# Attention and FFN on one core: softmax reciprocals turned one step later, two small jobs on GpSimd

## Chip, cores and metric

The program runs on one core of one Trainium2 chip. The metric is the device time of one execution in microseconds (us). Matmuls run on TensorE (PE; its weight loads are listed as PEld), elementwise work on VectorE (DVE), ScalarE (ACT) and GpSimd (POOL), transfers are issued by SyncE (SP).

## The reference, cut to what matters

```python
scores = scale * np.matmul(q, k.transpose(0, 1, 3, 2))        # batch 4, heads 8, seq 576, head 64
scores = scores + bias.transpose(2, 0, 1)[None]               # bias from a small MLP of the positions
scores = scores - np.max(scores, axis=-1, keepdims=True)
attn = np.exp(scores)
attn = attn / (np.sum(attn, axis=-1, keepdims=True) + 1e-09)
x = np.matmul(attn, v)                                        # -> 2304 tokens x 512
h = x @ w_in                                                  # 512 x 2048
return np.maximum(0.01 * h, h) @ w_out                        # 2048 x 512
```

## The kernel before

The program has three stages: the bias tables (to about 55 us), attention (to about 317 us) and the FFN. The change is in attention, which works on 16 units, one for each of 4 head pairs (`hp`) and 4 batches (`b`), in this order. A unit has nine tiles of scores, `KINDS = A0, B0, A1, B1, M, A2, B2, A3, B3`: A and B are the two heads, the digit a block of 128 queries, and M holds the last 64 queries of both heads. The order of everything is written out by hand: `step(n)` issues the work for tile n, and engines run their own instructions in that order.

For tile n of a step, `qk_mm` makes the scores on PE (L235, for M L227), `softmax_a` adds the bias and takes the row's extreme on DVE (L258, a custom instruction and a small one that reads its accumulator), and `softmax_b` takes the exponential and its row sum `sm` on ACT (L266). Three steps later (`LAG = 3`) `transposes` turns the tile on PE (L300; its last 128 columns go into a tile `ps_o`, L304 or L318), and ACT copies the result into `PT` (L316, L306).

The scaling by 1/(sum + 1e-9) comes last, since the product is computed transposed. `recip` runs once for each half of a unit, a step after M (half g = 0) and a step after B3 (half g = 1): DVE adds 1e-9 (L272), takes the reciprocal (L273), and GpSimd spreads it over columns in `rb` (L276, L278) and, for M, copies 64 columns of `pM` (L279). `turn_rb` turns `rb` on PE into columns 256 to 511 of `ps_o` (L289, for M also L305), and DVE copies it to `PT` (L290, for M before it two half copies, L309). `pv` is the product with V, 20 matmuls of half a unit (L335). It writes columns 0 to 287 of the same `ps_o` tile that L290 reads. `pv_exit` multiplies the product by the reciprocals on DVE (L344, L348).

In this text "the first turn" is `turn_rb` of half 0 and "the first product" the `pv` of half 0, which stands in the step of the next unit's A0; "the second turn" and "the second product" are those of half 1. The second product stands in the next unit's M step, where transposes and product go ahead of the scores (`ahead`); in all other steps the scores come first.

The FFN takes x in two parts, a rounded high part `xh` and the remainder `xl`. For the first block of 512 tokens, which are those of batch 0 (units 0, 4, 8 and 12, counted from 0), the split is made inside attention: ACT rounds as `pv_exit` runs (L345) and DVE subtracts one step later (L386). That is eight pieces, of 288 and 224 columns. Between these jobs GpSimd makes the low parts of q and k for the next unit (`split_lo`, L206 and L209), and DVE their high parts (L194, L199) and some of the weights' preparation (`fill`, L432 to L448).

Of the kernel before, what the change touches and what calls it, by code (L numbers as in the profile page):

```python
# [8 lines left out]
F32 = mybir.dt.float32  # L9
# [5 lines left out]
B, H, S, D, HID = 4, 8, 576, 64, 32  # L15
# [10 lines left out]
KINDS = ["A0", "B0", "A1", "B1", "M", "A2", "B2", "A3", "B3"]  # L26
# [3 lines left out]
LAG = 3  # L30
# [6 lines left out]
def attention_ffn(ctx: ExitStack, tc: tile.TileContext, qt, kt, vm, vt, wi, wo, cst, out):  # L37
    nc = tc.nc
# [18 lines left out]
    ident = ap.tile([128, 128], F32, name="ident")  # L57
# [7 lines left out]
    PT = ap.tile([128, 2, 10, HS], F32, name="PT")  # L65
# [27 lines left out]
    for T in GEN:  # L93
        w = gen_w(T)
# [116 lines left out]
    st, pp = {}, {}  # L211

    def tile_id(n):
        u, i = divmod(n, 9)
        return u, KINDS[i]
# [24 lines left out]
    def softmax_a(n):  # L240
        u, kind = tile_id(n)
        hp = u // B
        bt = bias[hp, "M"][:] if kind == "M" else bias[hp, kind[1]][:, 0 if kind[0] == "A" else 1, :]
        col = 1 if kind[0] == "B" else 0
        if col == 0:
            mx_t[n] = ap.tile([128, 2], F32, tag="mx", name="mx", bufs=6)
        else:
            mx_t[n] = mx_t[n - 1]
        g, sc = int(KINDS.index(kind) > 4), 4 if kind == "M" else 2 * (int(kind[1]) % 2) + col
        if kind in ("A0", "A2"):  # L250
            sm_t[u, g] = ap.tile([128, 12], F32, tag="sm", name="sm", bufs=3)
        if kind == "M":
            pair[0] = ap.tile([128, S + 64], F32, tag="pM", name="pM", bufs=1)
        elif col == 0:
            pair[0] = ap.tile([128, 2 * S], F32, tag="p", name="p", bufs=3)
        p = pair[0][:, S * col:S * col + S]
        s_, i = st.pop(n), mx_t[n][:, col:col + 1]
        nc.vector.tensor_tensor_reduce(out=p, in0=s_[:, S0:S0 + S], in1=bt, scale=-0.125, scalar=3.4e38, op0=ALU.add, op1=ALU.min, accum_out=i)  # L258
        pp[n] = pair[0]
        ex_q.append((p, i, sm_t[u, g][:, sc:sc + 1]))  # L260
# [3 lines left out]
    def softmax_b():  # L264
        p, i, sm = ex_q.pop(0)
        nc.scalar.activation(out=p, in_=p, func=AF.Exp, bias=i, scale=-1.0, accum_out=sm)  # L266

    def recip(n):
        u, kind = tile_id(n)
        g = int(kind != "M")  # L270
        sm, w = sm_t.pop((u, g)), 4 if g else 5
        nc.vector.tensor_scalar_add(sm[:, 0:w], sm[:, 0:w], 1e-9)  # L272
        nc.vector.reciprocal(sm[:, 6:6 + w], sm[:, 0:w])  # L273
        rb = rb_t[u, g] = ap.tile([128, 384], F32, tag="rb", name="rb", bufs=2)
        one = sm[:, 6:10].rearrange("p (h o) -> p h o", o=1).to_broadcast([128, 4, 64])
        nc.gpsimd.tensor_copy(rb[:, 0:256].rearrange("p (h c) -> p h c", h=4), one)  # L276
        if g == 0:
            nc.gpsimd.tensor_copy(rb[:, 256:384], sm[:, 10:11].to_broadcast([128, 128]))  # L278
            nc.gpsimd.tensor_copy(pp[n][:, S:S + 64], pp[n][:, S - 64:S])  # L279

    outs = {}
    pv_q = []

    def halves(t):
        return t[:].rearrange("p (a c) -> p a c", a=2)

    def turn_rb(u, g, rb):
        for i in range(2):
            nc.tensor.transpose(outs[u, g][:, 256 + 128 * i:384 + 128 * i], rb[:, 128 * i:128 * i + 128], ident[:])  # L289
        nc.vector.tensor_copy(PT[:, g, 8:10, 0:256], halves(outs[u, g]))  # L290

    def transposes(n, at):
        u, kind = tile_id(n)
        p = pp.pop(n)
        p0 = S + 64 if kind[0] == "B" else 0
        if kind in ("A0", "M"):
            outs[u, int(kind == "M")] = pstile("o")
        t0 = pstile("t")
        for jb in range(4):
            nc.tensor.transpose(t0[:, 128 * jb:128 * jb + 128], p[:, p0 + 128 * jb:p0 + 128 * jb + 128], ident[:])  # L300
        if kind == "M":
            rb = rb_t.pop((u, 0))
            tl = outs[u, 1]
            nc.tensor.transpose(tl[:, 0:128], p[:, 512:640], ident[:])  # L304
            nc.tensor.transpose(tl[:, 256:384], rb[:, 256:384], ident[:])  # L305
            nc.scalar.copy(out=PT[:, :, 0:8, 256:288], in_=t0[:].rearrange("p (j g c) -> p g j c", j=8, g=2))  # L306
            for h in range(2):
                r, c = slice(64 * h, 64 * h + 64), slice(64 * h, 64 * h + 64)
                nc.vector.tensor_copy(PT[r, :, 8:10, 256:288], halves(tl)[r, :, c].rearrange("p a (g c) -> p g a c", g=2))  # L309
            turn_rb(u, 0, rb)  # L310
            pv_q.append((at, u, 0))
            return
        ic, h = int(kind[1]), 0 if kind[0] == "A" else 1
        g, i2 = ic // 2, ic % 2
        c = slice(128 * i2, 128 * i2 + 128)
        nc.scalar.copy(out=PT[:, g, 0:8, c].rearrange("p (j h) c -> p j h c", h=2)[:, :, h, :], in_=t0[:].rearrange("p (j c) -> p j c", j=4))  # L316
        if h == 1:
            nc.tensor.transpose(outs[u, g][:, c], p[:, 512:640], ident[:])  # L318
            if kind == "B3":
                turn_rb(u, 1, rb_t.pop((u, 1)))  # L320
                pv_q.append((at, u, 1))

    x_pend, pv_out = [], []

# [13 lines left out]
    def pv_exit():  # L338
        hp, t0, o, r = pv_out.pop(0)
        c = max(0, min(HS, BLK - t0))  # L340
        if c:
            x = ap.tile([128, HS], F32, tag="xt", name="xt", bufs=2)
            hi, lo = (t[:, t0:t0 + c] for t in xs[0, hp])
            nc.vector.tensor_mul(x[:, 0:c], o[:, 0:c], r[:, 0:c])  # L344
            nc.scalar.copy(out=hi, in_=x[:, 0:c])  # L345
            x_pend.append((lo, x[:, 0:c], hi))
        if c < HS:
            nc.vector.tensor_mul(x1[hp][:, t0 + c - BLK:t0 + HS - BLK], o[:, c:HS], r[:, c:HS])  # L348

    NTILE = 9 * HP * B  # L350

# [13 lines left out]
    def step(n):  # L365
        ahead = n % 9 == 4
        for turn in (ahead, not ahead):
            if turn:
                if 0 <= n - LAG < NTILE:
                    transposes(n - LAG, n + 2)  # L370
                if pv_q and pv_q[0][0] <= n:
                    pv()
                continue
            if n < NTILE:
                qk_mm(n)
                if ahead and n // 9 + 2 < HP * B:
                    load_unit(n // 9 + 2)
                if ahead:
                    split(n, "M")
                    fill(n, 3)  # L380
                softmax_a(n)
            if 0 <= n - 1 < NTILE and KINDS[(n - 1) % 9] in ("M", "B3"):
                recip(n - 1)
            while x_pend:
                lo, x, hi = x_pend.pop(0)
                nc.vector.tensor_sub(lo, x, hi.bitcast(F32))  # L386
            while pv_out and not ahead:
                pv_exit()
        while ex_q:
            softmax_b()  # L390
# [258 lines left out]
```

## Time and profile before

| | |
|---|---|
| median of 3 runs (lowest to highest) | 720.21 us (719.26 to 720.31) |
| the profiled execution: time, span | 719.8 us, 718.0 us |
| busy share of the span: PE, PEld, DVE, ACT, POOL | 97%, 76%, 54%, 50%, 16% |
| granted TensorE clock, mean over the span | 1.000 of full speed |

The profile is of one execution. "Busy" is time in which an engine had an instruction under way; a PE matmul's end is modelled, so what counts for PE is where its instructions start. A remark in brackets behind a row, as [0.20 <-POOL pM L279], is idle time of that engine just before it, and what ended it.

### The profile page before, as it was taken

The numbers are of one execution on the slowest core, as the hardware profiler recorded it, in microseconds if no ns is written. First come the engines' busy times: TensorE is split into PE (matmuls) and PEld (weight loads), VectorE is DVE, ScalarE is ACT, GpSimd is POOL, SyncE is SP. The second block draws the span as 40 slices with busy tenths as digits, with TensorE's granted clock in tenths as the row PEclk, the third lists the DMA queues.
The fourth block names the chain that finished last, engine by engine and source line by source line (L and its number), as shares of the span: only waits on it lengthen the run. The fifth ranks groups of instructions, "written<-read, shape, count | busy, mean of one in ns | idle before, by whom it ended". The sixth has DMA issues, their size and how long they took to land.

```text
span 718.0 us, 11142 instructions
## 1 busy us (share of the span) xinstructions
PE 698.7 (97%) x4192; PEld 544.2 (76%) x4192; DVE 388.8 (54%) x882; ACT 362.6 (50%) x792; POOL 111.9 (16%) x135
## 2 busy tenths in 40 slices
PE   6999999999999999999999999999999999999997
PEld 2346677777767786767888888888888888888996
DVE  7996789898889889749996211122111221112111
ACT  7797778767778777775563221222211231122221
POOL 2103335333444434300000000000000000000000
PEclk9999999999999999999999999999999999999999
DMA  9798557447755864002550010000000010000100
GB/s 231 239 316 243 167 164 226 115 114 214 211 158 127 244 173 125 21 1 65 173 174 29 1 59 0 1 0 30 31 0 1 0 59 1 0 1 1 59 1 30
DMA packets 30262, 68.26 MB, mean 95 GB/s; under 512 B 8192, under 2 KB 8320, under 8 KB 30208
## 3 DMA queue, kind: packets, MB, share of 16 engines
q1 hardware_dynamic: 30208, 67.54, 32.4%
q8 instruction: 33, 0.54, 0.3%
q14 instruction: 21, 0.17, 0.1%
HBM read 51.92 MB, written 15.61 MB: 94 GB/s over the span
## 4 chain that ended last, share of the span: by engine, by line
PE 85%; DVE 9%; ACT 3%; issue 2%; DMA 1%; DVEq 0%; SPq 0%
PE ps_o L466 13%; PE ps_t L466 13%; PE ps_o L335 10%; PE ps_s L494 9%; PE ps_s L493 9%; PE ps_s L492 9%; PE ps_s L235 7%; PE ps_t L300 6%; DVE r L114 2%; PE ps_o L125 2%; PE ps_t L125 1%; DVE p L258 1%; PE ps_s L227 1%; PE ps_s L125 1%; DVE pM L258 1%
## 5 line engine op out<-in xcount | busy, mean ns | idle before, releaser
L481 DVE TENSOR_TENSOR gl<-g,gh 128x512 fp32r<-128x512 f32 (+1 forms) x80 | 51.0, 638 | 266.2 <-ACT g L475 266.2
L494 PE MATMUL ps_s<-woh,gl 128*128 128x512 f32 x288 | 112.1, 389 | 0.3 <-DVE gl L481 0.3
L492 PE MATMUL ps_s<-woh,gh 128*128 128x512 f32 x288 | 112.2, 390 | 0.0
L493 PE MATMUL ps_s<-wol,gh 128*128 128x512 f32 x288 | 112.2, 390 | 0.0
L266 ACT ACTIVATE p<-p,mx 128x576 f32<-128x576 f32 x128 | 100.0, 781 | 7.6 <-DVE mx L258 7.6
L258 DVE CUSTOM_DVE_ANT_0 p<-ps_s,bias 128x576 f32<-128x576 f32 x128 | 94.0, 750 | 15.0 <-PE ps_s L235 12.5
L235 PE MATMUL ps_s<-ks,qs 128*128 128x288 f32 x512 | 99.9, 318 | 1.8 <-DVE mx L258 1.5
L235 PEld LDWEIGHTS ps_s<-ks,qs 128*128 128x128 f32 x512 | 72.1, 189 | 19.5 <-issue 6.0
L474 ACT ACTIVATE gh<-ps_o 128x512 fp32r<-128x512 f32 (+1 forms) x39 | 21.5, 552 | 126.6 <-PE ps_o L466 126.6
L316 ACT COPY PT<-ps_t 128x512 f32<-128x512 f32 x128 | 73.4, 574 | 12.9 <-PE ps_t L300 12.9
L474 ACT ACTIVATE gh<-ps_t 128x512 fp32r<-128x512 f32 (+1 forms) x39 | 21.5, 552 | 112.0 <-PE ps_t L466 111.9
L300 PE MATMUL ps_t<-ident,p 128*128 128x128 f32 x512 | 75.0, 273 | 2.3 <-ACT PT L316 2.3
L335 PE MATMUL ps_o<-PT,v 128*64 128x288 f32 x512 | 69.2, 412 | 0.3
L300 PEld LDWEIGHTS ps_t<-ident,p 128*128 128x128 f32 x512 | 61.1, 140 | 4.5 <-ACT PT L316 3.6
L494 PEld LDWEIGHTS ps_s<-woh,gl 128*128 128x128 f32 x288 | 54.1, 188 | 12.0 <-DVE gl L481 0.7
L492 PEld LDWEIGHTS ps_s<-woh,gh 128*128 128x128 f32 x288 | 54.1, 188 | 10.8
L493 PEld LDWEIGHTS ps_s<-wol,gh 128*128 128x128 f32 x288 | 54.1, 188 | 10.6
L466 PE MATMUL ps_t<-xh,wil 128*128 128x512 f32 (+1 forms) x156 | 57.3, 367 | 0.0
L466 PE MATMUL ps_o<-xh,wil 128*128 128x512 f32 (+1 forms) x156 | 57.3, 367 | 0.0
L466 PE MATMUL ps_t<-xl,wih 128*128 128x512 f32 (+1 forms) x156 | 57.3, 367 | 0.0
L466 PE MATMUL ps_o<-xl,wih 128*128 128x512 f32 (+1 forms) x156 | 57.3, 367 | 0.0
L466 PE MATMUL ps_t<-xh,wih 128*128 128x512 f32 (+1 forms) x156 | 57.2, 367 | 0.0
(109 smaller groups left out, 1098.8 us busy)
## 6 DMA issues: line engine op xcount, KB each, us to landing
raw<-kt SPq DMA_DIRECT2D x32, 304.0 KB, 5.7
raw<-qt SPq DMA_DIRECT2D x32, 288.0 KB, 4.2
raw<-wi SPq DMA_DIRECT2D x16, 512.0 KB, 3.5
raw<-wo SPq DMA_DIRECT2D x16, 512.0 KB, 3.6
scr<-x SPq DMA_DIRECT2D x21, 295.5 KB, 4.2
bias<-scr SPq DMA_DIRECT2D x16, 288.0 KB, 5.4
out<-x SPq DMA_DIRECT2D x18, 256.0 KB, 2.1
v<-vm SPq DMA_DIRECT2D x16, 256.0 KB, 6.3
```

Source lines behind the costliest of these rows:

```text
L235: nc.tensor.matmul(s_[:, S0 + HS * hh:S0 + HS * hh + HS], qs[:, c0:c0 + 128], ks[:, k0 + HS * hh:k0 + HS * hh + HS], start=(j == 0), stop= ...
L258: nc.vector.tensor_tensor_reduce(out=p, in0=s_[:, S0:S0 + S], in1=bt, scale=-0.125, scalar=3.4e38, op0=ALU.add, op1=ALU.min, accum_out=i)
L266: nc.scalar.activation(out=p, in_=p, func=AF.Exp, bias=i, scale=-1.0, accum_out=sm)
L300: nc.tensor.transpose(t0[:, 128 * jb:128 * jb + 128], p[:, p0 + 128 * jb:p0 + 128 * jb + 128], ident[:])
L316: nc.scalar.copy(out=PT[:, g, 0:8, c].rearrange("p (j h) c -> p j h c", h=2)[:, :, h, :], in_=t0[:].rearrange("p (j c) -> p j c", j=4))
L335: nc.tensor.matmul(o[64 * h:64 * h + 64, 0:HS], l, r, start=(jb == 0), stop=(jb == 4))
L466: nc.tensor.matmul(h_[:, :N], w, x[:, :N], start=(j == 0), stop=(j == len(mms) - 1))
L474: nc.scalar.activation(out=gh[:, :N], in_=h_[:, :N], func=AF.Prelu, alpha=0.01)
L481: nc.vector.tensor_sub(gl[:, :N], g[:, :N], gh[:, :N].bitcast(F32))
L492: nc.tensor.matmul(o, gh[:, c], wt[m][2][:], start=(m == 0), stop=False)
L493: nc.tensor.matmul(o, gh[:, c], wt[m][3][:], start=False, stop=False)
L494: nc.tensor.matmul(o, gl[:, c], wt[m][2][:], start=False, stop=(m == MF - 1))
```

## The change

The addition of 1e-9 leaves DVE for GpSimd and gets a function of its own, `sums`, in the step in which it stood; the copy of the 64 columns of `pM` goes with it and so comes ahead of the spreading. `recip` (now the reciprocal and the spreading) runs two steps after M and B3 instead of one. `turn_rb` runs one step after the tile's other transposes instead of in the same step; the products keep their steps. For the first block, ACT's rounding moves to the next step (`x_steps`), and the subtraction goes from DVE to GpSimd, another step later.

```diff
@@ -265,18 +265,24 @@
         p, i, sm = ex_q.pop(0)
         nc.scalar.activation(out=p, in_=p, func=AF.Exp, bias=i, scale=-1.0, accum_out=sm)
 
+    def sums(n):
+        u, kind = tile_id(n)
+        g = int(kind != "M")
+        sm, w = sm_t[u, g], 4 if g else 5
+        nc.gpsimd.tensor_scalar_add(sm[:, 0:w], sm[:, 0:w], 1e-9)
+        if g == 0:
+            nc.gpsimd.tensor_copy(pp[n][:, S:S + 64], pp[n][:, S - 64:S])
+
     def recip(n):
         u, kind = tile_id(n)
         g = int(kind != "M")
         sm, w = sm_t.pop((u, g)), 4 if g else 5
-        nc.vector.tensor_scalar_add(sm[:, 0:w], sm[:, 0:w], 1e-9)
         nc.vector.reciprocal(sm[:, 6:6 + w], sm[:, 0:w])
         rb = rb_t[u, g] = ap.tile([128, 384], F32, tag="rb", name="rb", bufs=2)
         one = sm[:, 6:10].rearrange("p (h o) -> p h o", o=1).to_broadcast([128, 4, 64])
         nc.gpsimd.tensor_copy(rb[:, 0:256].rearrange("p (h c) -> p h c", h=4), one)
         if g == 0:
             nc.gpsimd.tensor_copy(rb[:, 256:384], sm[:, 10:11].to_broadcast([128, 128]))
-            nc.gpsimd.tensor_copy(pp[n][:, S:S + 64], pp[n][:, S - 64:S])
 
     outs = {}
     pv_q = []
@@ -284,12 +290,22 @@
     def halves(t):
         return t[:].rearrange("p (a c) -> p a c", a=2)
 
-    def turn_rb(u, g, rb):
+    def turn_rb(n, at):
+        u, kind = tile_id(n)
+        g = int(kind != "M")
+        rb = rb_t.pop((u, g))
+        if g == 0:
+            tl = outs[u, 1]
+            nc.tensor.transpose(tl[:, 256:384], rb[:, 256:384], ident[:])
+            for h in range(2):
+                r, c = slice(64 * h, 64 * h + 64), slice(64 * h, 64 * h + 64)
+                nc.vector.tensor_copy(PT[r, :, 8:10, 256:288], halves(tl)[r, :, c].rearrange("p a (g c) -> p g a c", g=2))
         for i in range(2):
             nc.tensor.transpose(outs[u, g][:, 256 + 128 * i:384 + 128 * i], rb[:, 128 * i:128 * i + 128], ident[:])
         nc.vector.tensor_copy(PT[:, g, 8:10, 0:256], halves(outs[u, g]))
-
-    def transposes(n, at):
+        pv_q.append((at, u, g))
+
+    def transposes(n):
         u, kind = tile_id(n)
         p = pp.pop(n)
         p0 = S + 64 if kind[0] == "B" else 0
@@ -299,16 +315,8 @@
         for jb in range(4):
             nc.tensor.transpose(t0[:, 128 * jb:128 * jb + 128], p[:, p0 + 128 * jb:p0 + 128 * jb + 128], ident[:])
         if kind == "M":
-            rb = rb_t.pop((u, 0))
-            tl = outs[u, 1]
-            nc.tensor.transpose(tl[:, 0:128], p[:, 512:640], ident[:])
-            nc.tensor.transpose(tl[:, 256:384], rb[:, 256:384], ident[:])
+            nc.tensor.transpose(outs[u, 1][:, 0:128], p[:, 512:640], ident[:])
             nc.scalar.copy(out=PT[:, :, 0:8, 256:288], in_=t0[:].rearrange("p (j g c) -> p g j c", j=8, g=2))
-            for h in range(2):
-                r, c = slice(64 * h, 64 * h + 64), slice(64 * h, 64 * h + 64)
-                nc.vector.tensor_copy(PT[r, :, 8:10, 256:288], halves(tl)[r, :, c].rearrange("p a (g c) -> p g a c", g=2))
-            turn_rb(u, 0, rb)
-            pv_q.append((at, u, 0))
             return
         ic, h = int(kind[1]), 0 if kind[0] == "A" else 1
         g, i2 = ic // 2, ic % 2
@@ -316,9 +324,6 @@
         nc.scalar.copy(out=PT[:, g, 0:8, c].rearrange("p (j h) c -> p j h c", h=2)[:, :, h, :], in_=t0[:].rearrange("p (j c) -> p j c", j=4))
         if h == 1:
             nc.tensor.transpose(outs[u, g][:, c], p[:, 512:640], ident[:])
-            if kind == "B3":
-                turn_rb(u, 1, rb_t.pop((u, 1)))
-                pv_q.append((at, u, 1))
 
     x_pend, pv_out = [], []
 
@@ -342,10 +347,20 @@
             x = ap.tile([128, HS], F32, tag="xt", name="xt", bufs=2)
             hi, lo = (t[:, t0:t0 + c] for t in xs[0, hp])
             nc.vector.tensor_mul(x[:, 0:c], o[:, 0:c], r[:, 0:c])
-            nc.scalar.copy(out=hi, in_=x[:, 0:c])
             x_pend.append((lo, x[:, 0:c], hi))
         if c < HS:
             nc.vector.tensor_mul(x1[hp][:, t0 + c - BLK:t0 + HS - BLK], o[:, c:HS], r[:, c:HS])
+
+    x_lo = []
+
+    def x_steps(n):
+        while x_lo:
+            lo, x, hi = x_lo.pop(0)
+            nc.gpsimd.tensor_sub(lo, x, hi.bitcast(F32))
+        while x_pend:
+            lo, x, hi = x_pend.pop(0)
+            nc.scalar.copy(out=hi, in_=x)
+            x_lo.append((lo, x, hi))
 
     NTILE = 9 * HP * B
 
@@ -367,7 +382,9 @@
         for turn in (ahead, not ahead):
             if turn:
                 if 0 <= n - LAG < NTILE:
-                    transposes(n - LAG, n + 2)
+                    transposes(n - LAG)
+                if 0 <= n - LAG - 1 < NTILE and KINDS[(n - LAG - 1) % 9] in ("M", "B3"):
+                    turn_rb(n - LAG - 1, n + 1)
                 if pv_q and pv_q[0][0] <= n:
                     pv()
                 continue
@@ -379,11 +396,11 @@
                     split(n, "M")
                     fill(n, 3)
                 softmax_a(n)
+            if 0 <= n - 2 < NTILE and KINDS[(n - 2) % 9] in ("M", "B3"):
+                recip(n - 2)
             if 0 <= n - 1 < NTILE and KINDS[(n - 1) % 9] in ("M", "B3"):
-                recip(n - 1)
-            while x_pend:
-                lo, x, hi = x_pend.pop(0)
-                nc.vector.tensor_sub(lo, x, hi.bitcast(F32))
+                sums(n - 1)
+            x_steps(n)
             while pv_out and not ahead:
                 pv_exit()
         while ex_q:
```

How this moves instructions shows at three places. The first is DVE's order around the second turn of one unit, in the next unit's steps B0 to M. `qs` and `ks` are the high parts of q and k, `x` the scaled product, `mx` the accumulator, `tmp` weights in preparation. Before:

```order
L348 TENSOR_TENSOR x_1_70<-ps_o,PT 128x288
L194 CAST qs_101<-raw_84 128x1024
L258 ISA p,mx<-ps_s,bias 128x576
L258 ISA mx 128x1
L290 COPY PT<-ps_o 128x2x256
L258 ISA p,mx<-ps_s,bias 128x576
L258 ISA mx 128x1
L199 CAST ks_2032<-raw_85 128x1216
```

The same place now, where the numbers of the lines are those of the changed file (L352 was L348, L305 was L290):

```order
L352 TENSOR_TENSOR x_1_70<-ps_o,PT 128x288
L194 CAST qs_101<-raw_84 128x1024
L258 ISA p,mx<-ps_s,bias 128x576
L258 ISA mx 128x1
L258 ISA p,mx<-ps_s,bias 128x576
L258 ISA mx 128x1
L305 COPY PT<-ps_o 128x2x256
L199 CAST ks_2032<-raw_85 128x1216
```

The copy of the reciprocals to `PT` has changed places with the softmax instruction of tile B1; the reciprocal of this half, which stood some instructions earlier, now stands just ahead of the first row.

The second place is PE's order around the same turn, from the scores of tile B1 to the product. Before, with the two transposes of `rb` ahead of those scores:

```order
L289 MATMUL ps_o<-ident,rb 128x128 x2
L235 MATMUL ps_s<-ks_2455,qs_101 128x288 x2
L235 MATMUL ps_s<-ks_2456,qs_101 128x288 x2
L300 MATMUL ps_t<-ident,p 128x128 x8
L318 MATMUL ps_o<-ident,p 128x128
L335 MATMUL ps_o<-PT,v 64x288 x8
```

And now (L316 was L300, L326 was L318, L304 was L289, L340 was L335):

```order
L235 MATMUL ps_s<-ks_2455,qs_101 128x288 x2
L235 MATMUL ps_s<-ks_2456,qs_101 128x288 x2
L316 MATMUL ps_t<-ident,p 128x128 x4
L304 MATMUL ps_o<-ident,rb 128x128 x2
L316 MATMUL ps_t<-ident,p 128x128 x4
L326 MATMUL ps_o<-ident,p 128x128
```

Between the turn and the product stood four matmuls of scores and nine transposes, and now five transposes; the row of the product follows.

The third place is GpSimd's order, from the M tile of one unit to the first piece of `xl` in the next but one step. Before:

```order
L276 COPY rb<-sm 128x256
L278 COPY rb<-sm 128x128
L279 COPY pM<-pM 128x64
L209 TENSOR_TENSOR ks_1621<-raw_85,ks_1620 128x576
L209 TENSOR_TENSOR ks_1621<-raw_85,ks_1620 128x640
L276 COPY rb<-sm 128x256
L206 TENSOR_TENSOR qs_100<-raw_82,qs_100 64x512 x2
```

And now:

```order
L272 TENSOR_SCALAR sm<-sm 128x5
L274 COPY pM<-pM 128x64
L209 TENSOR_TENSOR ks_1621<-raw_85,ks_1620 128x576
L283 COPY rb<-sm 128x256
L285 COPY rb<-sm 128x128
L209 TENSOR_TENSOR ks_1621<-raw_85,ks_1620 128x640
L272 TENSOR_SCALAR sm<-sm 128x4
L283 COPY rb<-sm 128x256
L206 TENSOR_TENSOR qs_100<-raw_82,qs_100 64x512
L359 TENSOR_TENSOR xl_902<-xt,xh_901 128x288
L206 TENSOR_TENSOR qs_100<-raw_82,qs_100 64x512
```

The spreading into `rb` has moved behind the first of the two pieces of k's low part, and the copy of `pM` ahead of it; the two additions and a subtraction are new on this engine.

## Rows read from the trace of the kernel before

**Rows 1.** Busy time by stretch, two units: us, then each engine, PEclk, DMA, GB/s.

```profile
117.74:133.51 15.77, 15.77 (x129) 12.23 (x130) 13.55 (x35) 12.58 (x31) 6.95 (x9) 1.00 0.72 207
133.51:151.31 17.80, 16.50 (x129) 12.23 (x130) 15.65 (x37) 12.60 (x31) 7.45 (x9) 1.00 0.51 126
```

**Rows 2.** Chain that ended last, products and one DVE piece: start, us, what.

```profile
117.74 2.58 PE ps_o L335 x20
...
124.30 2.58 PE ps_o L335 x20
...
133.51 2.58 PE ps_o L335 x20
...
139.26 1.15 DVE xl L386
...
141.07 2.65 PE ps_o L335 x20
...
151.31 2.58 PE ps_o L335 x20
```

**Rows 3.** Timeline around a second turn: start, us, engine, line, operation.

```profile
170.60 0.76 DVE L258 CUSTOM_DVE_ANT_0 p<-ps_s,bias 128x576 f32<-128x576 f32 x1 [1.24 <-PE ps_s L235]
...
171.29 0.45 DVE L348 TENSOR_TENSOR x<-ps_o,PT 128x288 f32<-128x288 f32 x1
...
171.66 0.68 DVE L194 CAST qs<-raw 128x1024 fp32r<-128x1024 f32 x1
...
172.25 0.75 DVE L258 CUSTOM_DVE_ANT_0 p<-ps_s,bias 128x576 f32<-128x576 f32 x1
...
172.93 0.68 DVE L290 COPY PT<-ps_o 128x512 f32<-128x512 f32 x1
...
173.75 1.17 PEld L335 LDWEIGHTS ps_o<-PT,v 128*64 128x64 f32 x12 [0.17 <-DVE PT L290]
```

**Rows 4.** Line L335, what its weight loads waited for: us, times.

```profile
  DVE PT L290: 3.9, 19
```

**Rows 5.** Timeline around a first turn.

```profile
113.66 0.17 DVE L272 TENSOR_SCALAR sm<-sm 128x5 f32<-128x5 f32 x1 [0.26 <-ACT pM L266]
...
114.18 0.40 POOL L276 COPY rb<-sm 128x256 f32<-128x256 f32 x1 [4.38 <-DVE sm L273]
...
114.75 0.24 POOL L279 COPY pM<-pM 128x64 f32<-128x64 f32 x1
...
114.95 2.96 POOL L209 TENSOR_TENSOR ks<-raw,ks 128x576 fp32r<-128x576 f32 x2
...
115.05 0.14 PEld L304 LDWEIGHTS ps_o<-ident,pM 128*128 128x128 f32 x1 [0.20 <-POOL pM L279]
...
115.44 0.56 PEld L235 LDWEIGHTS ps_s<-ks,qs 128*128 128x128 f32 x4
...
117.67 1.65 PEld L335 LDWEIGHTS ps_o<-PT,v 128*64 128x64 f32 x16 [0.17 <-DVE mx L258]
```

**Rows 6.** Groups by line and shape, 54 to 330 us: busy us, mean ns.

```profile
L209 POOL TENSOR_TENSOR ks<-raw,ks 128x576 fp32r<-128x576 f32 x15 | 21.4, 1428 | 0.0
...
L273 DVE RECIPROCAL sm<-sm 128x5 f32<-128x5 f32 x16 | 3.0, 189 | 0.5
```

**Rows 7.** Timeline, DVE instructions that overlap a GpSimd instruction.

```profile
147.65 1.58 DVE L386 TENSOR_TENSOR xl<-xt,xh 128x224 fp32r<-128x224 f32 x1
...
153.26 0.70 POOL L276 COPY rb<-sm 128x256 f32<-128x256 f32 x1 [2.60 <-DVE sm L273]
153.62 0.62 DVE L432 TENSOR_SCALAR tmp<-tmp 128x512 f32<-128x512 f32 x1
...
168.44 0.40 DVE L432 TENSOR_SCALAR tmp<-tmp 128x512 f32<-128x512 f32 x1
```

**Rows 8.** Timeline, a unit whose M tile comes late from DVE.

```profile
162.29 0.56 PEld L235 LDWEIGHTS ps_s<-ks,qs 128*128 128x128 f32 x4 [0.29 <-DVE mx L258]
```

**Rows 9.** Chain that ended last, the piece behind the last product.

```profile
322.70 0.68 DVE wil L448
```

## Prediction

> **What bounds the kernel now.** I read the busy time by stretch first, since the change lies in attention alone. A unit in the middle of attention, from one first product to the next, takes 15.77 us, and PE is busy in all of it [rows 1]. The unit behind it takes 17.80 us with PE busy for 16.50 us: it is one in which the first block's low parts are made. So a plain unit is set by PE's order, and an instruction that comes later on PE's way makes the unit longer, unless something else there gets shorter.
>
> The chain that ended last, read second, splits the units into two windows. Window A goes from the first product to the second, window B from the second to the next first. In the plain unit they take 124.30 - 117.74 = 6.56 us and 133.51 - 124.30 = 9.21 us [rows 2]. In the unit with the low parts they take 7.56 us and 10.24 us: 1.00 and 1.03 us more, with the subtraction (1.15 us) on the chain in the first. These pairs of windows come once for each head pair, so there are 4 x 2.03 = 8.1 us to be had from the low parts.
>
> The timeline around a second turn, read third, shows how close DVE is behind PE. DVE waits for the scores of tile B0 until 170.60, works without a pause through softmax, x, qs, softmax, and ends the copy of the reciprocals at 172.93 + 0.68 = 173.61; the product's first weight load starts at 173.75 [rows 3]. Elsewhere a product shows the same 0.17 us before its load where nothing binds, as in [rows 5], so here DVE's copy has some 0.08 us of slack. The product's loads waited for this copy 19 times, 3.9 us in all, 0.2 us each [rows 4]: a wait that is just met, not one with room. It can't be left out, because the product overwrites the columns that the copy reads.
>
> **The change, part by part.**
>
> *The second turn* is the largest term. On DVE the copy now stands behind the softmax of B1 instead of ahead of it, and the reciprocal, which stood earlier, now stands in this stretch. The softmax costs 172.93 - 172.25 = 0.68 us [rows 3]. The reciprocal's instruction lasts 0.19 us, but DVE's next one starts before it ends; I take 0.10 us (bounds 0.10 to 0.19) [rows 6]. With 0.08 us of slack the product starts 0.68 + 0.10 - 0.08 = 0.70 us later. PE has nothing to put there: its next instruction in order is the product itself, and behind it stand the M tile's scores.
>
> To this comes GpSimd's spreading, which follows the reciprocal and now runs as DVE comes to the cast of q (it ran earlier, beside the weights' work). The instruction of L432 takes 0.40 us alone and 0.62 us when a spreading started 0.36 us before it, and that spreading 0.70 us instead of 0.40 us; the subtraction L386, 224 columns, took 1.58 us beside a piece of k of 1.43 us [rows 5, 6, 7]. So each of the two engines can hold the other up. I take 0.15 us, with bounds of 0 (they miss each other) and 0.40 us (the whole spreading). The second turn then costs 0.70 + 0.15 = 0.85 us.
>
> The Trainium skill has a rule for this (SBUF — State Buffer, "Who interferes with whom"): of a GpSimd instruction and a DVE instruction in a mode that uses both ports, the one that starts first keeps the shared pair to its end and the other waits fully. The trace agrees with it in the 0.62 us of rows 7. By the rule alone, with the cast due about 0.16 us into the spreading, the wait would be an estimated 0.24 us rather than 0.15 us, and the time 0.9 us longer than mine.
>
> There are 15 second turns inside attention (the 16th is at the tail). Four are in windows with a low part; the one of the last unit but one has no cast of q beside it (there is no unit to prepare), and I give it 0.3 us. The other ten give 10 x 0.85 = 8.5 us.
>
> *The first turn* loses something and gains something. Before, PE waited 0.20 us for the copy of pM, which was third in GpSimd's queue [rows 5]. Now that copy is second, behind the addition, and is long done. PE also has three transposes less at that place, so the scores of B3 start at 115.44 - 0.45 = 114.99 (0.20 us of wait and 0.25 us of weight loads). But the spreading now stands behind a piece of k of 1.43 us [rows 6]. I reckon it through in the times of [rows 5]: the row sums of M are ready at about 113.6 (DVE's addition started at 113.66). GpSimd's addition has no row; the nearest is the copy of 64 columns, 0.24 us, and its bounds are 0.10 us (almost nothing) and 0.70 us (the longest spreading [rows 7]). Addition, copy and piece of k end at 113.66 + 0.24 + 0.20 + 1.43 = 115.53, and the two spreadings, 114.75 - 114.18 = 0.57 us, at 116.10. PE wants them at about 115.98 and turns them by 116.6. DVE's two half copies and the full copy behind them take 0.62 + 0.69 = 1.31 us, and so the product's load starts at 117.98 instead of 117.67. With the rounding of these rows I take 0.33 us, bounds 0.20 us (then the softmax of B3 sets DVE's start) and 0.79 us. All 16 first turns pay, four of them in windows with a low part: 12 x 0.33 = 4.0 us.
>
> *The low parts.* The subtraction leaves DVE, the rounding no longer makes ACT wait in its place, and the GpSimd pieces (288 columns, about half the piece of k, so 0.7 us) stand between or behind jobs that the next unit wants only steps later. Their windows become plain windows of the new kind: four times 0.85 - 1.00 = -0.15 us and four times 0.33 - 1.03 = -0.70 us, together -3.4 us. The larger part of the 8.1 us is thus spent on the later turns.
>
> *The additions on DVE* (0.17 us, with 0.26 us of waiting for ACT ahead [rows 5]) are worth nothing in themselves: in the steps where they stand, DVE waits afterwards for PE anyway (1.24 us before the first row of [rows 3]). If that cover were gone, 32 times 0.43 us would be 13.8 us at most.
>
> *The tail.* The last second turn now stands behind the FFN's first twelve matmuls instead of ahead of them, and these no longer cover its copy: 0.68 us for the copy and about 0.3 us for the turn itself, less 0.25 us that the matmuls start earlier, 0.7 us. DVE's work behind the last product is on the chain [rows 9], so this passes on.
>
> *What the delay gives back.* In three units DVE comes late to the M tile, and PE waits for it, as the 0.29 us of [rows 8]. With the product 0.85 us later this wait is covered: -3 x 0.29 = -0.9 us.
>
> **Sum.** 8.5 + 0.3 + 4.0 - 3.4 + 0.7 - 0.9 = +9.2 us on the profiled execution's 719.8 us, 729.0 us. That execution is 0.4 us below the median of the runs shown, so the forecast is 729.4 us. With the low bounds of all prices (0.70, 0.1, 0.20, 0.4 at the tail) the sum is 7.0 + 0.1 + 2.4 - 1.2 - 3.3 + 0.4 - 0.9 = +4.5 us, 724.7 us; with the high ones (1.10, 0.5, 0.79, 0.9, and no more than 0.3 given back) 11.0 + 0.5 + 9.5 + 0.4 - 1.0 + 0.9 - 0.3 = +21.0 us, 741.2 us.
>
> **The rivals.**
>
> *Faster: the turns stay hidden.* If a product did not have to wait for the copy of the reciprocals, the change would keep all of its gains: 8.1 us from the low parts and 16 x 0.20 = 3.2 us from the waits for pM, 719.8 - 11.3 + 0.4 = 708.9 us. It decides on whether the first weight load of a product starts before the copy ends. For it speaks that in plain units the copy is not on the chain; against it the 19 waits of [rows 4], and that the slack I read is 0.08 us. A rule speaks for it too. The Trainium skill (Perfetto Trace Analysis, "Identifying the Most-Contended Engine") says that matmul busy time is a poor measure of how full TensorE is, and that weight loads' busy share is a better one. By that rule the 12.23 us of loads in 15.77 us [rows 1] leave 22% free, and a later product could be caught up. The chain bears it out badly: PE is in order, and work that is only free in the mean cannot move ahead of a waiting product. Chance 0.10.
>
> *A wash.* The later turns cost less than half of what I take, because PE's work behind a late product runs with fewer waits than now. With 0.35 and 0.10 us for the turns and 0.5 us at the tail the terms are 3.5 + 0.1 + 1.2 - 2.6 - 3.7 + 0.5 - 0.9 = -1.9 us; with a little more they meet zero: 718 to 722 us, 720 us in the middle. Against it: those units show no idle PE that could go. Chance 0.10.
>
> *Heavier: GpSimd is the new bound of the first turn.* If the small addition costs as much as the longest spreading, or the piece of k is held up by DVE, the first turns take the high price and the port the whole spreading: up to 741 us. For it: spreadings of 0.70 us occur. Against: most take 0.40 us. Chance 0.12.
>
> **How the numbers follow.** The forecast's mechanism with moderate prices, 724.7 to 737 us, has the remaining 0.68. About 0.2% (1.4 us) is what a measurement of this kernel can tell from no change. Slower takes 0.68 + 0.12 + 0.03 of the wash, 0.83; the same 0.05; faster 0.10 + 0.02, 0.12. The range from 722 to 738 us leaves out the faster rival, half of the wash and most of the heavier one, some 2 in 10.
>
> **What would show it.** In the new profile the second products' loads should show 0.7 to 1.0 us of waiting for the copy L305 in window A, some 7.4 us long in all units, and the first products' loads 0.2 to 0.4 us with windows B near 9.5 us. The subtraction should be off the chain, and the pM transposes (L318) show no wait. If window A stays at 6.6 us in plain units, the step on the second turn is wrong. If the loads of the spreading's transposes (L299) wait a microsecond for GpSimd, the price of the addition is.

## The result, and the profile after

The changed kernel takes 730.52 us (median of 4 runs, 729.77 to 731.17) against 719.80 us of the kernel before (median of 4): a ratio of 1.0149 with an interval of 1.0131 to 1.0166. It is slower, within 1.1 us of the forecast of 729.4 us. The profiled execution took 729.77 us with a span of 728.0 us, 10.0 us more than before's 718.0 us.

The line of the page on busy time (each engine's busy us, share of the span, instructions) shows no engine that became full. PE has its 4192 instructions and 0.1 us less of busy time than before (698.7 us), in a span that is 10 us longer:

```profile
PE 698.6 (96%) x4192; PEld 544.2 (75%) x4192; DVE 380.4 (52%) x842; ACT 361.9 (50%) x792; POOL 127.2 (17%) x175
```

Busy time by stretch, for the same two units as [rows 1], plain and with low parts (length, then PE, PEld, DVE, ACT, POOL, granted clock, DMA share, GB/s):

```profile
119.62:136.52 16.90, 15.82 (x126) 12.21 (x126) 13.44 (x33) 12.57 (x30) 7.55 (x10) 1.00 0.66 191
136.52:153.60 17.08, 16.42 (x127) 12.21 (x127) 14.84 (x35) 12.39 (x31) 9.11 (x12) 1.00 0.49 124
```

The plain unit grew from 15.77 to 16.90 us while PE's busy time stayed: 1.1 us of PE are now empty in each. The unit with the low parts fell from 17.80 to 17.08 us. The two are now nearly alike, as the prediction said.

The chain that ended last, in the stretch that answers to [rows 2] (start, us, what):

```profile
124.14 0.81 DVE qs L194
...
126.31 0.61 DVE PT L305
126.96 2.65 PE ps_o L340 x20
...
132.54 0.24 POOL pM L274
...
134.10 0.40 POOL rb L283
...
135.16 0.28 DVE PT L302
135.45 0.29 DVE PT L302
135.78 0.70 DVE PT L305
136.52 2.65 PE ps_o L340 x20
...
143.22 0.61 DVE PT L305
143.87 2.65 PE ps_o L340 x20
```

Where PE followed PE from product to product, the chain now leaves PE ahead of every product: for DVE's cast of q, a softmax and the copy of the reciprocals ahead of a second product (126.96), for GpSimd's queue and three copies on DVE ahead of a first one (136.52). The subtraction is gone from it. The page's line of the products' weight loads, which answers to [rows 4] (busy us, mean ns, idle us before them, and what ended most of it):

```profile
L340 PEld LDWEIGHTS ps_o<-PT,v 128*64 128x64 f32 x512 | 34.1, 136 | 38.9 <-DVE PT L305 19.0
```

Of the loads' 38.9 us of idle time, 19.0 us in 31 waits ended with this copy; it was 3.9 us in 19 waits. The load of the pM transposes (L318) shows no wait at all.

The timeline around a second turn, as [rows 3]:

```profile
124.01 0.40 POOL L283 COPY rb<-sm 128x256 f32<-128x256 f32 x1 [3.09 <-PE ps_s L235]
124.14 0.81 DVE L194 CAST qs<-raw 128x1024 fp32r<-128x1024 f32 x1
124.88 0.74 DVE L258 CUSTOM_DVE_ANT_0 p<-ps_s,bias 128x576 f32<-128x576 f32 x1
125.55 0.75 DVE L258 CUSTOM_DVE_ANT_0 p<-ps_s,bias 128x576 f32<-128x576 f32 x1
126.23 0.68 DVE L305 COPY PT<-ps_o 128x512 f32<-128x512 f32 x1
126.96 1.17 PEld L340 LDWEIGHTS ps_o<-PT,v 128*64 128x64 f32 x12 [0.97 <-DVE PT L305]
```

DVE works without a pause, as before, but two softmaxes now stand between the cast and the copy, where one stood in [rows 3], and PE waits 0.97 us where a load shows 0.17 us when nothing binds. The cast takes 0.81 us, with a spreading that started 0.13 us before it, against 0.68 us in [rows 3]; over all 15 casts the mean went from 0.683 to 0.803 us.

The timeline around a first turn, as [rows 5]:

```profile
132.24 0.24 POOL L272 TENSOR_SCALAR sm<-sm 128x5 f32<-128x5 f32 x1 [4.54 <-ACT pM L266]
132.54 0.24 POOL L274 COPY pM<-pM 128x64 f32<-128x64 f32 x1
132.73 1.43 POOL L209 TENSOR_TENSOR ks<-raw,ks 128x576 fp32r<-128x576 f32 x1
...
134.10 0.40 POOL L283 COPY rb<-sm 128x256 f32<-128x256 f32 x1
...
134.79 0.14 PEld L299 LDWEIGHTS ps_o<-ident,rb 128*128 128x128 f32 x1 [0.48 <-POOL rb L285]
```

GpSimd's addition, which had no row before, costs 0.24 us. The reciprocals were there at 132.9 us (DVE's L280 ran from 132.75 for 0.18 us), but the spreading starts at 134.10: the piece of k is in its way.

All windows of the two traces, from product's load to product's load, added up by the terms of the prediction (us; unit 0 to 15 are the head pairs in order):

| windows | number | before | after | sum of differences | predicted |
|---|---|---|---|---|---|
| A of plain units | 10 | 6.56 (unit 1: 6.71) | 7.35 (unit 1: 7.57) | +8.03 | +8.5 |
| A of unit 14 (no cast of q) | 1 | 6.56 | 6.88 | +0.32 | +0.3 |
| B of plain units, and unit 14's | 8 | 9.21 (14: 8.83) | 9.56 (14: 9.22) | +2.86 | 12 x 0.33 - 0.9 = +3.1 for these three rows |
| B of the units 1, 5, 10 (late M tile) | 3 | 9.44 | 9.57 | +0.37 | (above) |
| start of attention to the first product | 1 | 67.9 (load) | 68.7 | +0.82 | (above) |
| A and B with a low part | 4 + 4 | 7.63, 10.16 | 7.34, 9.61 | -1.17 - 2.19 = -3.36 | -3.4 |
| A of unit 15 (tail) | 1 | 6.70 | 7.61 | +0.91 | +0.7 |
| sum | | | | +9.95 | +9.2 |

### The profile page after: what moved, and what is told of

It reads as the page before. It is cut to its first block, busy times and chain, and to the rows that moved or that the text cites. A ratio compares the mean times of both kernels' runs of the same rounds, so it can differ in the third digit from the quotient of the medians.

```text
span 728.0 us, 11173 instructions
## 1 busy us (share of the span) xinstructions
PE 698.6 (96%) x4192; PEld 544.2 (75%) x4192; DVE 380.4 (52%) x842; ACT 361.9 (50%) x792; POOL 127.2 (17%) x175
## 4 chain that ended last, share of the span: by engine, by line
PE 77%; DVE 11%; DMA 5%; issue 4%; ACT 2%; POOL 1%; SPq 0%; DVEq 0%; POOLq 0%; ACTq 0%
PE ps_o L483 13%; PE ps_t L483 13%; PE ps_o L340 11%; PE ps_s L511 9%; PE ps_s L509 9%; PE ps_s L510 9%; PE ps_s L235 4%; DMA bias<-scr 3%; DVE PT L305 3%; PE ps_t L316 2%; DVE r L114 2%; DVE p L258 2%; PE ps_o L125 2%; PE ps_s L227 1%; DVE qs L194 1%
## 5 line engine op out<-in xcount | busy, mean ns | idle before, releaser
L235 PE MATMUL ps_s<-ks,qs 128*128 128x288 f32 x512 | 99.7, 317 | 1.1 <-DVE mx L258 1.1
L235 PEld LDWEIGHTS ps_s<-ks,qs 128*128 128x128 f32 x512 | 72.1, 189 | 16.2 <-issue 13.8
L340 PE MATMUL ps_o<-PT,v 128*64 128x288 f32 x512 | 69.2, 412 | 12.6 <-DVE PT L305 11.0
L316 PE MATMUL ps_t<-ident,p 128*128 128x128 f32 x512 | 77.0, 274 | 0.5 <-ACT PT L324 0.3
L316 PEld LDWEIGHTS ps_t<-ident,p 128*128 128x128 f32 x512 | 61.2, 140 | 3.4 <-ACT PT L324 2.5
L340 PEld LDWEIGHTS ps_o<-PT,v 128*64 128x64 f32 x512 | 34.1, 136 | 38.9 <-DVE PT L305 19.0
```

Of the source, the lines that this page charges most:

```text
L235: nc.tensor.matmul(s_[:, S0 + HS * hh:S0 + HS * hh + HS], qs[:, c0:c0 + 128], ks[:, k0 + HS * hh:k0 + HS * hh + HS], start=(j == 0), stop= ...
L340: nc.tensor.matmul(o[64 * h:64 * h + 64, 0:HS], l, r, start=(jb == 0), stop=(jb == 4))
```

## The experiments

The theory: each second product waits for a copy that DVE now reaches one softmax later, each first product for spreadings that stand behind a piece of k on GpSimd, and together they cost more than the low parts bring. The rivals are that the low parts bring less than 8.1 us by themselves, that the terms don't add up, and for the first turn that DVE's copies, not GpSimd's queue, set its end.

### e1_low_parts: the kernel before, with the low-part edit alone

```diff
             nc.vector.tensor_mul(x[:, 0:c], o[:, 0:c], r[:, 0:c])
-            nc.scalar.copy(out=hi, in_=x[:, 0:c])
             x_pend.append((lo, x[:, 0:c], hi))
...
-            while x_pend:
-                lo, x, hi = x_pend.pop(0)
-                nc.vector.tensor_sub(lo, x, hi.bitcast(F32))
+            x_steps(n)
```

> Only the first block's part of the change: rounding a step later, subtraction on GpSimd; additions, reciprocals and turns as before. Theory (the loss is DVE's order at the two turns, the low parts are a gain of 4 x 2.03 us that the change also has): windows A and B of all units become those of the plain units, 6.56 and 9.21 us, and the time is 720 - 8 = 712 us. Rival (GpSimd's extra work is what costs, by holding up DVE): the four windows A with a subtraction on GpSimd stay near 7.6 us, and the time is 716 us or more.

Measured: 714.1 us (713.81 to 714.32), ratio 0.9917 (0.9902 to 0.9932). The time lies between the theory's 712 us and the rival's 716 us. The edit is a gain alone, of 5.8 us, but 2.3 us short of the 8.1. Windows A of the four units fell to 6.75 us, 0.2 us above plain ones, and windows B of units 4 and 12 only to 9.66 and 9.55 us instead of 9.21. The timeline in unit 4:

```profile
139.34 0.80 POOL L354 TENSOR_TENSOR xl<-xt,xh 128x288 fp32r<-128x288 f32 x1
...
140.22 1.70 POOL L206 TENSOR_TENSOR qs<-raw,qs 64x512 fp32r<-64x512 f32 x1
...
140.71 1.49 DVE L440 TENSOR_SCALAR tmp<-tmp 128x512 f32<-128x512 f32 x1
...
144.12 0.56 PEld L235 LDWEIGHTS ps_s<-ks,qs 128*128 128x128 f32 x4 [0.55 <-DVE mx L258]
```

The subtraction pushes q's second low piece (L206) into the time of DVE's work on the FFN's weights. The weights' instruction takes 1.49 us, where [rows 7] have it at 0.40 us alone, and ends 0.28 us after the GpSimd piece. The softmax of the M tile comes late behind it, and PE waits 0.55 us. Window A of unit 1 grew to 7.94 us, since ACT there waits for the weights' transfer:

```profile
88.71 0.68 ACT L433 ACTIVATE tmp<-raw 128x512 f32<-128x512 f32 x1 [1.10 <-DMA raw<-wo]
```

So the rival's mechanism, GpSimd holding up DVE, is there, in two of the four units and at a smaller price.

### e2_turns_only: the changed kernel, with the low-part edit undone

The diff of e1 the other way round, in the changed kernel.

> The changed kernel with the first block's part taken back: rounding at once and the subtraction on DVE a step later; the additions on GpSimd and the later reciprocals and turns stay. Theory: gains and losses add up, so the four window pairs with a subtraction are longer by the 2.0 us each that they were longer before, windows A about 8.4 us and B about 10.5 us there, and the time is 730.5 + 8 = 738.5 us. Rival (a product that waits for the later copy anyway covers the subtraction): those windows stay near 7.6 and 10.2 us, and the time is 732 to 734 us.

Measured: 737.89 us (735.51 to 740.66), ratio 1.025 (1.0217 to 1.0284). Windows A with the low part are 8.43 to 8.51 us: the second turn's price and the subtraction add up. Windows B with it are 10.08 us, not 10.5 (unit 8's is 11.77 us, by the dip shown below): in unit 4 the subtraction runs on DVE from 152.42 for 1.49 us, while the spreading stands in GpSimd's queue until 154.40, so the two partly cover each other. The runs differ by 5 us, with a mean granted clock of 1.0 in the shortest and 0.995 in the longest. The profiled run (737.75 us, clock 0.997) has one dip; busy time by stretch, columns as above:

```profile
214.00:216.00 2.00, 0.94 (x7) 0.71 (x9) 2.00 (x5) 2.00 (x6) 1.62 (x2) 0.98 0.02 4
216.00:218.00 2.00, 2.00 (x10) 1.03 (x10) 1.23 (x3) 1.18 (x4) 0.00 (x0) 0.50 0.00 0
218.00:220.00 2.00, 2.00 (x12) 0.86 (x8) 0.00 (x0) 0.00 (x0) 0.00 (x0) 0.67 0.00 0
220.00:222.00 2.00, 2.00 (x20) 1.48 (x19) 1.10 (x3) 0.24 (x1) 0.00 (x0) 1.00 0.00 0
```

After a stretch with PE busy for 0.94 of 2 us the granted clock fell to 0.50 (1.2 GHz) and came back to 1.00 (2.4 GHz) by 220 us; the window with the product in between took 1.7 us longer than its like (11.77 against 10.08 us).

### e3_second_early: the second turn at the head of its step

```diff
         ahead = n % 9 == 4
+        if 0 <= n - LAG - 1 < NTILE and KINDS[(n - LAG - 1) % 9] == "B3":
+            turn_rb(n - LAG - 1, n + 1)
...
-                if 0 <= n - LAG - 1 < NTILE and KINDS[(n - LAG - 1) % 9] in ("M", "B3"):
+                if 0 <= n - LAG - 1 < NTILE and KINDS[(n - LAG - 1) % 9] == "M":
                     turn_rb(n - LAG - 1, n + 1)
```

> The changed kernel with the second turn alone moved ahead of the scores of tile B1, at the head of its step; reciprocals, spreading and additions stay where the change put them, and GpSimd's list of work is the same. Theory (DVE's copy behind the softmax of B1 is the cost): windows A go from 7.35 back to 6.6 to 6.75 us (a rest for the reciprocal and for the cast that meets the spreading), windows B stay at 9.56 us, and the time is 730.5 - 15 x 0.65 = 721 us. Rival (GpSimd's spreading in that window and the port are the cost): windows A stay above 7.1 us and the time above 727 us.

Measured: 724.81 us (723.62 to 726.31), ratio 1.0067 (1.0048 to 1.0086). The timeline around the second turn has the softmax behind the copy again, and the product's load without a wait:

```profile
123.50 0.20 PEld L304 LDWEIGHTS ps_o<-ident,rb 128*128 128x128 f32 x2 [0.20 <-POOL rb L283]
...
124.59 0.68 DVE L305 COPY PT<-ps_o 128x512 f32<-128x512 f32 x1
...
125.19 0.74 DVE L258 CUSTOM_DVE_ANT_0 p<-ps_s,bias 128x576 f32<-128x576 f32 x1
...
125.38 1.65 PEld L340 LDWEIGHTS ps_o<-PT,v 128*64 128x64 f32 x16 [0.17 <-DVE PT L305]
...
143.24 1.49 DVE L451 TENSOR_SCALAR tmp<-tmp 128x512 f32<-128x512 f32 x1
...
146.65 0.56 PEld L235 LDWEIGHTS ps_s<-ks,qs 128*128 128x128 f32 x4 [0.73 <-DVE mx L258]
```

Plain windows A are 6.72 to 6.73 us, those with a low part 6.76 us. So 0.62 us of the second turn's price come from its place in the order, as predicted. The edit moves PE's two transposes along with DVE's copy; but in the changed kernel PE had them done in time (they start at 125.20), and the copy came only at 126.23, right behind the softmax, so it is DVE's order that counts. The rest, up to before's 6.56 us, is not the one that the expectation names: the first row shows PE at the turn waiting 0.20 us for GpSimd's spreading, which the later reciprocal makes late. Such waits come 14 times in this trace and never in that of the changed kernel, where PE reaches the turn later.

The time stays 3.8 us above the expected 721, and the last two rows, from unit 4, show one place of it: with the product on time, PE meets the late M tile again, here behind the weights' instruction of 1.49 us. Windows B grew in units 1, 5 and 10 by 0.27, 0.34 and 0.31 us against the changed kernel, which is the 0.9 us that the prediction said the delay gives back. They grew in units 4 and 12, too, from 9.73 and 9.59 us to 10.31 and 10.19 us, by the collision of e1. Unit 1's window A is 7.95 us by the weights' transfer. I had counted none of these in the expectation.

### e4_k_behind: k's first low piece behind the spreading

```diff
-SPL = {1: [(0, "q")], 2: [(1, "q", 0)], 3: [(1, "q", 1)], "M": [(0, "k")], 5: [(1, "k", 0)], 6: [(1, "k", 1)]}
+SPL = {1: [(0, "q")], 2: [(1, "q", 0)], 3: [(1, "q", 1)], "M": [(0, "k")], 6: [(1, "k", 0), (1, "k", 1)]}
```

> The changed kernel with the first piece of k's low part moved behind the spreading of the first turn, so that both pieces follow it. Theory (GpSimd's queue costs PE 0.24 us at the turn, but DVE's softmax of B3 and its three copies bind the product right after): PE's wait for the spreading goes, windows B go from 9.56 to about 9.42 us only, and the time is 730.5 - 15 x 0.14 = 728.4 us. Rival (the piece of k ahead of the spreading is all of the cost of the first turn): windows B go back to 9.21 us and the time to 725.3 us.

Measured: 726.64 us (726.37 to 727.47), ratio 1.0094 (1.0079 to 1.0109), and plain windows B of 9.22 to 9.23 us: the rival's number for the windows. The time is 1.3 us above the rival's, which counted 15 equal windows: those with a low part got only 0.22 to 0.25 us shorter, unit 14's none, and window A of unit 1 grew by 0.26 us. The timeline around a first turn:

```profile
117.57 0.40 POOL L283 COPY rb<-sm 128x256 f32<-128x256 f32 x1 [0.29 <-PE ps_s L235]
...
118.17 2.94 POOL L209 TENSOR_TENSOR ks<-raw,ks 128x576 fp32r<-128x576 f32 x2
...
118.78 0.14 PEld L299 LDWEIGHTS ps_o<-ident,rb 128*128 128x128 f32 x1
...
119.65 0.30 PEld L235 LDWEIGHTS ps_s<-ks,qs 128*128 128x128 f32 x2 [0.25 <-POOL ks L209]
...
119.95 0.69 DVE L305 COPY PT<-ps_o 128x512 f32<-128x512 f32 x1
...
120.69 1.65 PEld L340 LDWEIGHTS ps_o<-PT,v 128*64 128x64 f32 x16 [0.19 <-DVE PT L305]
```

The load of the turns waits for nothing, and the product's load shows 0.19 us instead of 0.35. Of the 0.35 us that a plain window B had grown, 0.33 were k's place in GpSimd's queue. The new place has a price of its own: the next unit's scores now wait 0.25 us for the late piece (L235), in ten units. The copies on DVE, which follow the softmax without a pause, end together with what that wait delays, so the two costs do not add.

### e5_both_eased: e3 and e4 together

The two diffs above in one kernel.

> The changed kernel with both turns eased at once: the second turn at the head of its step, and both pieces of k's low part behind the first turn's spreading. Additions, reciprocals and subtraction stay on their new engines and in their new steps. Theory (the two turns' places in the orders are the whole loss): windows A at 6.7 us, windows B at 9.23 us but where DVE comes late to the M tile (up to 0.7 us in five units), the tail still 0.9 us longer, and the time is 724.8 - 15 x 0.33 = 719.9 us. Rival (the eased turns get in each other's way, or GpSimd's work costs by itself): windows B stay above 9.5 us in plain units, and the time is 723 us or more.

Measured: 719.31 us (10 runs, 718.75 to 721.62), ratio 1.0 (0.9991 to 1.0009). The two places take back all that the change had lost. What the low parts bring is still spent: on the tail (window A of unit 15 is 7.61 us), on windows A that stay 0.2 us above before's 6.56 us (by the wait for the spreading, as in e3, 14 times here too), on windows B of 10.08 and 9.97 us in units 4 and 12, on 0.8 us more in unit 1's window A.

### e6_low_pm: e1, with the copy of pM first in GpSimd's queue

```diff
+        if g == 0:
+            nc.gpsimd.tensor_copy(pp[n][:, S:S + 64], pp[n][:, S - 64:S])
         nc.vector.tensor_scalar_add(sm[:, 0:w], sm[:, 0:w], 1e-9)
...
         if g == 0:
             nc.gpsimd.tensor_copy(rb[:, 256:384], sm[:, 10:11].to_broadcast([128, 128]))
-            nc.gpsimd.tensor_copy(pp[n][:, S:S + 64], pp[n][:, S - 64:S])
```

> The kernel before with the first block's part of the change and one thing more of it: the copy of pM's 64 columns stands ahead of the spreading in GpSimd's queue. Additions, reciprocals and turns are as before. Theory: PE's wait for that copy (0.20 us in each unit) goes, windows B are 9.0 us in plain units, and the time is 714.1 - 15 x 0.2 = 711.1 us. Rival (the spreading, now 0.2 us later, takes the wait's place at the next transposes): windows B stay at 9.2 us and the time at 714 us.

Measured: 711.81 us (711.28 to 712.33), ratio 0.989 (0.9874 to 0.9907). It is faster than both kernels. Around a first turn the turns' load waits for nothing, and PE goes to the product with 0.17 us:

```profile
128.95 2.96 POOL L209 TENSOR_TENSOR ks<-raw,ks 128x576 fp32r<-128x576 f32 x2
129.04 0.14 PEld L305 LDWEIGHTS ps_o<-ident,pM 128*128 128x128 f32 x1
...
131.71 0.93 PEld L336 LDWEIGHTS ps_o<-PT,v 128*64 128x64 f32 x10 [0.17 <-issue]
```

Plain windows B are 8.99 to 9.03 us, 0.2 us shorter than before: the 0.20 us that PE waited for pM in [rows 5] are to be had by one line's place, with nothing turned later.

### e7_low_pm_late and e8_low_pm_late2: e6, with the subtraction a step later still

Both are one and the same kernel. The subtraction waits in its list until q's second low piece has been issued, to take it out of the collision of e1.

```diff
-        while x_lo:
-            lo, x, hi = x_lo.pop(0)
-            nc.gpsimd.tensor_sub(lo, x, hi.bitcast(F32))
+        for _ in range(len(x_lo)):
+            m, lo, x, hi = x_lo.pop(0)
+            if m < n:
+                nc.gpsimd.tensor_sub(lo, x, hi.bitcast(F32))
+            else:
+                x_lo.append((m, lo, x, hi))
...
-            x_lo.append((lo, x, hi))
+            x_lo.append((n + 1, lo, x, hi))
```

> The same with the subtraction on GpSimd one step later still, behind the second piece of q's low part instead of between the two pieces. Theory (the subtraction pushes the second piece into the weights' work on DVE, where one instruction took 1.49 us instead of 0.40 us for the port, and the M tile comes late): the windows B behind a low part lose up to 0.4 us in two units, and the time is 0.5 to 1 us below that of the kernel with the subtraction between the pieces, 710.3 us. Rival (the weights' work itself is what makes the M tile late): the same time within 0.3 us.

Measured: 710.86, 711.12 and 711.59 us, and 2398.53 us for the profiled execution, with the same 4192 matmuls spread over all of it, so that its trace tells nothing of the edit. The same kernel once more:

> The kernel of the run before once more, for a profile of an undisturbed execution. Theory: windows B behind a low part are 9.0 to 9.2 us in the units in which they were 9.59 and 9.46 us with the subtraction between the pieces, the instruction of the weights' work that took 1.49 us takes 0.4 us, and the time is 711 us. Rival: those windows stay at 9.4 us or more.

Measured: 711.39 us (711.14 to 711.8), ratio 0.9881 (0.9865 to 0.9898). The timeline at the weights' instruction:

```profile
139.68 1.23 POOL L356 TENSOR_TENSOR xl<-xt,xh 128x288 fp32r<-128x288 f32 x1
...
140.18 1.02 DVE L444 TENSOR_SCALAR tmp<-tmp 128x512 f32<-128x512 f32 x1
```

The weights' instruction now meets the subtraction instead of the piece of q, and takes 1.02 instead of 1.49 us. Windows B of units 4 and 12 fell by 0.11 us each, to 9.48 and 9.35 us, where the theory had 9.0 to 9.2 us: the subtraction takes over more than half of the piece's part in the collision (0.62 of 1.09 us). The intervals of e6 and e8 overlap: the two can't be told apart by the time.

## Why the prediction was right, point by point

**The bound.** Right: PE's order sets a plain unit, and each of the later products made its unit longer by as much as it came late. The gain that the prediction drew for the faster rival from a rule of the Trainium skill (Perfetto Trace Analysis, "Identifying the Most-Contended Engine"), by which the weight loads' share is the better measure of how full TensorE is, did not come: with loads busy for 12.21 of 16.90 us nothing was caught up. The rule does not say that a late product can be caught up; that step was the prediction's own.

**The second turn.** Right in place and cause, as e3 shows by undoing it: 0.80 us in the mean of ten windows, where I took 0.85. The part of the meeting with GpSimd is 0.12 us (the cast's mean), where I took 0.15 from bounds of 0 and 0.40. The rule of the full wait (SBUF — State Buffer, "Who interferes with whom" in the Trainium skill) made it an estimated 0.24 us, more than the row. Worked out for all four meetings shown here, the rule is too high by nearly the same each time. The rest of the GpSimd instruction is 0.27 us for the cast, 0.34 us in [rows 7], 1.21 us in e1 and 0.73 us in e8; the DVE instruction got longer by 0.13, 0.22, 1.09 and 0.62 us, which is 0.11 to 0.14 us less.

**The first turn.** The size was right (0.35 us in plain windows, 0.33 predicted), and the working through GpSimd's queue as well. Wrong was its lower bound, 0.20 us if "the softmax of B3 sets DVE's start": in e4, with k's piece out of the way, the copies do start right behind that softmax, and the window is only 0.02 us longer than before. In the changed kernel unit 0 shows that bound's mechanism, at a larger price. There DVE is late by the bias transfer, and the softmax that it brings (66.68) is now ahead of the half copies:

```profile
66.68 0.76 DVE L258 CUSTOM_DVE_ANT_0 p<-ps_s,bias 128x576 f32<-128x576 f32 x1 [0.18 <-DMA bias<-scr]
...
67.36 0.59 DVE L302 COPY PT<-ps_o 64x128 f32<-64x128 f32 x2
67.98 0.69 DVE L305 COPY PT<-ps_o 128x512 f32<-128x512 f32 x1
```

Before, the half copies came ahead of the last softmax, at 66.50 us instead of 67.36; the first product came 0.82 us later than before, where I had counted 0.33. That is 0.5 us of the 0.75 by which the sum was short.

**The low parts.** The sum was right, -3.36 against -3.4 us, but by luck in part: windows A gave 1.17 us where the working has 4 x 0.15 = 0.6, windows B 2.19 us where it has 4 x 0.70 = 2.8, and the two errors cancel. The 8.1 us "to be had" were not: alone the edit brings 5.8 us (e1), for GpSimd's pieces collide with the weights' work and unit 1 then waits for its weights. In the changed kernel the late products hide most of that, which is why the plain windows predicted them well. That is no merit of the working: I had said that these pieces stand where the next unit wants them only steps later, and had not looked at what DVE does beside them. The first piece of k, too, is wanted at once when it comes later (e4).

**The tail** cost 0.91 us instead of 0.7. The last product's load shows where:

```profile
329.58 1.44 PEld L340 LDWEIGHTS ps_o<-PT,v 128*64 128x64 f32 x14 [1.08 <-ACT woh L461]
```

PE's loads stand for 1.08 us, against 0.35 us before. The row names ACT, but DVE's copy (L305) lies in that gap, from 328.77 for 0.69 us, and the product's first matmul waits for it. So 0.73 of the 0.91 us lie in that gap, with the copy uncovered, and the other 0.18 us ahead of it.

**What the delay gives back** was nearly right in the three units that I named: 0.9 us by e3, 0.7 us by the table (3 x 0.35 less 0.37). It hides another 1.2 us in units 4 and 12, which I had not seen.

**The rivals.** The faster one fell with the wait of 0.97 us in nine of the ten plain second turns (0.72 us in unit 1). The wash fell with both prices: 0.80 and 0.35 us, where it has 0.35 and 0.10. The heavy one rested on an addition of 0.70 us ahead of a first turn; it takes 0.24 us there. The additions of the second half (128x4) take 0.468 us in the mean, but one reciprocal alone waited for one (1.2 us, at the tail, with the FFN's matmuls still ahead of the turn).

Left open: the additions and the reciprocals on their own. No run moved them without the turns, so that they cost nothing else is read from the traces and from e5, which keeps them and takes before's time.

## What to carry to other kernels

"A step later" is no size: follow the moved instruction into the in-order queue of every engine that it touches, an idle one's too, and write down what stands ahead of it there. Here one piece of k on GpSimd, 17% busy, cost 0.33 us per unit, and one softmax on DVE 0.6 us. A wait that is just met (0.08 us) has no room, and PE, in its fixed order, caught up nothing that came late. Of two edits that travel together, measure each alone: one brought 5.8 us and the other took 18.

## What the runs showed of the hardware that I had not expected

In the profiled executions of e2 and e4 the granted clock fell once to 0.50 (1.2 GHz), and was back at 1.00 within 6 us, each time behind a stretch in which PE had waited (busy for 0.94 of 2 us in e2, for 1.21 and 1.23 of 2 us in e4); window B of unit 8 was 11.77 us instead of 10.08 in e2, and window A of unit 0 was 8.96 us instead of 7.28 in e4. Much the same waits passed without a dip elsewhere: 1.22 and 1.17 of 2 us in units 4 and 12 of e2, 1.44 and 1.23 of 2 us in the changed kernel at the place of e4's. What decides between them is not shown. The kernel with the most waits also has the widest spread (735.51 to 740.66 us in e2, 711.28 to 712.33 us in e6); that dips make it is only suggested, by the mean clocks of e2's runs. And a DVE instruction of 0.40 us on the weights took 1.49 us beside a GpSimd piece of 1.70 us, nearly the full wait: the price of a GpSimd instruction is not only its own.
